# Attention with a feed-forward block in float32: values placed ahead of the scores from step 45 on, and the exponents of the weights formed in one ScalarE operation

## The chip, the cores and the metric

The kernel runs on one core of a Trainium2 chip. The time is device microseconds of one execution, from the first to the last instruction with what lies around them; lower is better. Three runs of the kernel before gave 1533.35, 1534.32 and 1534.38 us. One further execution was recorded by the profiler, and all durations below come from it.

## What is computed

Two blocks follow one another. The first is attention in which every query keeps the keys with its 32 largest scores; the second takes the rows of its result through a feed-forward pair of weights with `h - tanh(h)` between them.

```python
B, H, S, D = 8, 8, 576, 64
scores = scale * np.matmul(q, k.transpose(0, 1, 3, 2))
kth = np.partition(scores, -32, axis=-1)[..., -32:-31]
scores = np.where(scores >= kth, scores, -1e9)
attn = np.exp(scores - np.max(scores, axis=-1, keepdims=True))
attn = attn / (np.sum(attn, axis=-1, keepdims=True) + 1e-09)
x = np.matmul(attn, v)                       # -> (4608, 512)
h = x @ w_in                                 # w_in  (512, 2048)
g = h - np.tanh(h)
out = g @ w_out                              # w_out (2048, 512)
```

q, k and v are float32. The two weight matrices arrive as float64, as the inputs are set up, and are turned into float32 on the chip from their raw words.

## The kernel before

**Steps.** The attention is cut into 144 steps. A step takes 128 queries of two heads at once (a head pair; `t` in the code tells the two apart) against all 576 keys. Since 576 is four blocks of 128 and a rest of 64, every second head pair adds a step for the rests of two head pairs. There are 18 steps per batch. Steps of one unit (256 queries of a batch, or the rests of two batches) together give the rows that the feed-forward block needs.

**A step through the engines.** The work of step n is spread over several turns of the loop in `run`:

- `scores(n)` (L238): TensorE multiplies Q and K, eight passes of 288 columns, into the one score buffer `scps` in PSUM; ScalarE copies it to `sc` (L246). The next scores may be written only when L246 and the two VectorE reads L268 and L269 are done.
- `search(n)`: VectorE finds the 32nd largest score per row (L268 to L279, some 9 us per step). Between its rounds other VectorE work is slipped in: the turning of K and Q (L223), of the weights `z` (L388), and the conversion of the feed-forward matrices.
- `mask(n)` (L295 to L315) on ScalarE and GpSimd takes away what is below the threshold, `expo(n)` (L331) takes the exponential, `divide(n)` (L357) divides by the sum, `turn_z` and `spread_keys` (L388, L403, L405) bring the weights into key order by a VectorE transpose and a round trip through DRAM. In the first batch TensorE does this instead (`turn_pe`, L425, L428).
- `values(m)` (L453) multiplies the turned weights with V: 20 passes of 256 columns into `av`, which ScalarE copies into `xT` (L473). It runs for the last step of a group, five turns after that step (`LAG`). When this completes a unit, `work.extend(ffn(u))` puts the unit's feed-forward items into a list.

**Feed-forward items.** An item is a short run of matmuls, 1.7 us on TensorE: `ffn_h` (L504) for `w_in`, after every second item followed by tanh and a copy on ScalarE (L516, L517) and a difference on GpSimd (L518); and `ffn_o` (L525) for `w_out`, after every eighth item followed by a copy (L535) and the DMA out. In each turn of the loop `rate()` computes from the length of the list, and from when units fall due, how many items the turn should take, and `deal(part)` issues that share in parts: 0.4 ahead of the scores, then 0.2, 0.2 and 0.2 after them.

**Shapes on TensorE.** Feed-forward matmuls use the whole array (128*128 in the profile's notation). Scores use two tiles of 64 rows (64*128), values two tiles of 64 columns (128*64), each pair side by side.

**Order.** The order of the instructions on every engine is the order in which this loop issues them; nothing is rearranged later. Each engine then works through its own list and waits by semaphores where it needs something from another.

**The conversion.** `convert` takes one of 32 pieces (128 x 512 elements) from float64 to float32. Two DMAs bring the raw words and the same bytes shifted. VectorE cuts out the exponent field (L158) and the mantissa (L164), ScalarE turns both into numbers (L159 and L162 the exponent, L167 the mantissa), VectorE puts sign and exponent together (L170), GpSimd multiplies (L173). The pieces are spread over the searches of steps 0 to 10: two each in steps 0 and 1, three each in 2 to 9, four in step 10. A piece's exponent is clamped to the range 0 to 255 by two rectifiers in a row:

```python
nc.scalar.activation(f[:], fu, AF.Relu, bias=e1151[:], scale=-(2.0**23))
nc.scalar.activation(e.bitcast(I32), f[:], AF.Relu, bias=e255[:], scale=-1.0)
```

The kernel holds a second copy of the whole loop, with an exact search, which runs only if a count taken at the end of the first is above zero.

Of the kernel before, what the change touches and what calls it, by code (L numbers as in the profile page):

```python
# [8 lines left out]
AF = mybir.ActivationFunctionType  # L9
ALU = mybir.AluOpType  # L10
FP32 = mybir.dt.float32
I32 = mybir.dt.int32
# [6 lines left out]
EPS = 1.0e-9  # L19
J = 4  # L20
LAG = 5


class Step:
# [4 lines left out]
    def __init__(self, b, hp, qt, unit, col, i=0, nq=1, pe=False):  # L29
# [4 lines left out]

        self.lag = 2 if pe else LAG

# [13 lines left out]
def kernel(  # L50
# [9 lines left out]
    nc = tc.nc  # L60
    P = nc.NUM_PARTITIONS
# [15 lines left out]
    scale = 1.0 / float(D) ** 0.5  # L77
# [5 lines left out]
    def pool(name, bufs, **kw):  # L83
        return ctx.enter_context(tc.tile_pool(name=name, bufs=bufs, **kw))

    consts = pool("consts", 1)
# [28 lines left out]
    zx1 = consts.tile([P, 4 * S], FP32, name="zx")[:]  # L115
    et2 = [consts.tile([P, 4 * S], FP32, name="et")[:], later[:, 0 : 4 * S]]
    et_rem = later[:, 4 * S : 6 * S]
    e1151 = consts.tile([P, 1], FP32, name="e1151")
    nc.gpsimd.memset(e1151[:], 1151.0 * 2.0**23)
    e255 = consts.tile([P, 1], FP32, name="e255")  # L120
    nc.gpsimd.memset(e255[:], 255.0 * 2.0**23)

    def flat(x):
        return x.rearrange("p n w -> p (n w)")
# [13 lines left out]
    def convert(piece, slot):  # L138


        j, i = piece // CD, piece % CD
        if j < WJ:
            src, dst = moe_w_in[i * P : (i + 1) * P, j * NW : (j + 1) * NW], w_in[j][:, i, :]
        else:
            r0 = ((j - WJ) * FJ + i) * P
            src, dst = moe_w_out[r0 : r0 + P, :], w_out[j - WJ][:, i, :]
        raw, shifted, _ = slot
        nc.sync.dma_start(flat(raw), src.bitcast(U32))
        nc.sync.dma_start(
            flat(shifted).bitcast(U8)[:, 0 : 8 * NW - 4], src.bitcast(U8)[:, 3 : 8 * NW - 1]  # L150
        )
        yield
        hi = raw[:, :, 1]
        f = thpool.tile([P, NW], FP32, tag="th", name="f")
        fu = f[:].bitcast(U32)


        nc.vector.tensor_scalar(fu, hi, 20, 0x7FF, ALU.logical_shift_right, ALU.bitwise_and)  # L158
        nc.scalar.activation(f[:], fu, AF.Relu, bias=e1151[:], scale=-(2.0**23))  # L159

        e = h_ps.tile([P, NW], FP32, tag="h", name="e")[:] if j < WJ else f[:]
        nc.scalar.activation(e.bitcast(I32), f[:], AF.Relu, bias=e255[:], scale=-1.0)  # L162

        nc.vector.tensor_scalar(  # L164
            dst.bitcast(U32), shifted[:, :, 0], 0x0FFFFFFF, None, ALU.bitwise_and
        )
        nc.scalar.activation(dst, dst.bitcast(U32), AF.Copy, bias=1.0, scale=2.0**-28)  # L167
        yield

        nc.vector.scalar_tensor_tensor(  # L170
            out=fu, in0=hi, scalar=0x80000000, in1=e.bitcast(U32), op0=ALU.bitwise_and, op1=ALU.bitwise_or
        )
        nc.gpsimd.tensor_tensor(dst, dst, f[:], ALU.mult)  # L173
        yield
# [9 lines left out]
    def half(t):  # L184
        return slice(t * D, (t + 1) * D)
# [192 lines left out]
    def tiles(x, nq):  # L378

        x = x[:, 0 : nq * 2 * S]  # L380
        return x.rearrange("p (a k i j) -> p a k i j", a=NG, k=KC, j=G)
# [53 lines left out]
    def in_order(x, nq):  # L435

        return x.rearrange("p (a i j) -> p i a j", a=NG, i=nq)

    def values(n):


        g = steps[n]
        nq, u = g.nq, g.unit
        et = tiles(ets.pop(n), nq)
        w = nq * P
        av = zt_ps.tile([P, 2, N], FP32, tag="zt", name="av")
        for i in range(2 if g.rem else 1):
            cols = half(i) if g.rem else slice(0, w)
            es = et[:, 2 * i : 2 * i + 2] if g.rem else et
            hp = g.hp + i  # L450
            for c in range(J + 1):
                for t in range(2):
                    nc.tensor.matmul(  # L453
                        av[half(t), 0, cols],
                        vb[g.b, hp][:, t, c, :] if c < J else vr[g.b, hp][:, t, :],
                        es[:, :, (J + 1) * t + c if c < J else J].rearrange("p a i j -> p a (i j)"),
                        start=(c == 0),
                        stop=(c == J),
                    )
        if g.pe:  # L460
            rx = rxs.pop(n)
            for i in range(nq):
                nc.tensor.transpose(
                    in_order(av[:, 1, 0:w], nq)[:, i], rx[:, i].rearrange("p t d -> p (t d)"), ident[:]
                )
            xs = xrpool.tile([P, 2, N], FP32, tag="xs", name="xs")
            nc.scalar.copy(xs[:, :, 0:w], av[:, :, 0:w])

        def put(dst, order, cols):
            if g.pe:  # L470
                nc.gpsimd.tensor_tensor(dst, order(xs[:, 0, cols]), order(xs[:, 1, cols]), ALU.mult)
            else:
                nc.scalar.copy(dst, order(av[:, 0, cols]))  # L473

        if g.rem:
            for i in range(2):
                put(xt(u)[:, g.hp + i, g.col : g.col + R], lambda x: x, half(i))
        else:
            dst = xt(u)[:, g.hp, g.col : g.col + w].rearrange("p (i a j) -> p i a j", a=NG, i=nq)
            put(dst, lambda x: in_order(x, nq), slice(0, w))  # L480
        if n in done:
            work.extend(ffn(u))
# [3 lines left out]
    def xt(u):  # L486
        if u.xT is None:
            p = xpool if u.tag == "xT" else xrpool
            u.xT = p.tile([P, CD, N], FP32, tag=u.tag, name=u.tag)
        return u.xT  # L490
# [48 lines left out]
    def ffn(u):  # L539

        nh = CF * u.n // (2 * P)
        for item in range(nh):
            f = (item + 1) * CF // nh - 1
            yield CD * (f // FJ + 1), u, lambda item=item: ffn_h(u, item)
        for i in range(len(u.blocks)):
            for part in range(CF // 2):
                yield CD * (WJ + part // 2 + 1), None, lambda i=i, part=part: ffn_o(u, i, part)
# [3 lines left out]
    steps, done, work = [], {}, []  # L551
# [36 lines left out]
    def run(exact):  # L588
        plan()
        NS = len(steps)  # L590
# [7 lines left out]
        for i, (b, hp) in enumerate(pairs):  # L598
            n = next(n for n, g in enumerate(steps) if (g.b, g.hp) == (b, hp))
            for x, name in enumerate("kq"):  # L600
                m = max(n - 5 + x, turned.get(name, -4))
                if b == 0 and not exact:
                    m = -4
# [52 lines left out]
        def here(i):  # L656
            return 0 <= n + i < NS
# [26 lines left out]
        def rate():  # L684


            have, low, high = len(work), 0.0, None
            coming = sorted((t, u.n // 8) for u, t in ready.items() if t > n)
            for t, k in coming + [(NS + LAG, 0)]:
                r = have / max(t - n, 1)  # L690
                high = r if high is None else min(high, r)
                have += k
            for u, t in begun.items():
                if t > n and u in before:
                    need = [i + 1 for i, x in enumerate(work) if x[1] is before[u]]
                    if need:
                        low = max(low, need[-1] / (t - n))
            return max(low, high)
# [3 lines left out]
        def deal(part):  # L702
            nonlocal credit
            credit += part * share
            while work and credit > 0 and work[0][0] <= usable:
                work.pop(0)[2]()
                credit -= 1
            credit = min(credit, 1.0)

        for n in range(-4, NS + LAG):  # L710
            pe = here(-2) and steps[n - 2].pe
            for m in (n - LAG, n - LAG + 1, n - LAG + 2):
                if 0 <= m < NS and steps[m].last and steps[m].lag == n - m:
                    values(m)
            share, usable = rate(), converted[0]
            if pe:
                w = turn_pe(n - 2)
                next(w)
            if here(-1):
                mask(n - 1, exact)  # L720
            if here(0):
                search(n, exact, between)
            elif here(-2):
                between(0)
                between(LATE)
            if here(-2) and not pe and steps[n - 2].last:
                spread_keys(n - 2)
            if pe:
                spread(n - 2)
            deal(0.0 if pe else 0.4)  # L730
            if here(1):
                scores(n + 1)
            if pe:
                next(w)
            if here(-1):
                expo(n - 1)
            deal(0.8 if pe else 0.2)
            if pe and steps[n - 2].last:
                values(n - 2)
            deal(0.0 if pe else 0.2)  # L740
            for fn in todo.pop(n, []):
                fn()
            deal(0.2)
# [48 lines left out]
```

## Time and profile before

| | us |
|---|---|
| median of three runs | 1534.32 |
| the profiled execution | 1534.82 |
| its span (first to last instruction) | 1533.0 |
| TensorE (PE) busy | 1432.2 |
| VectorE (DVE) busy | 1349.9 |
| ScalarE (ACT) busy | 1021.6 |
| GpSimd (POOL) busy | 871.3 |
| last scores (step 143) begin on TensorE | 1408.59 |

How to read it: busy times overlap, so they don't add up to the span. A row of slices gives the busy share in 40 equal parts of the span, some 38 us each, in tenths. In the chain of waits each line is a piece of the work that ended last, with its start, its length and how many instructions it holds. PEld is the loading of weights into the array, which can lie beside matmuls. In a list of waits a line names the waiting instruction, what released it, the total, how often, and the longest.

### The profile page before, as it was taken

How to read it: one execution, taken by the hardware profiler on the slowest of the kernel's cores; microseconds unless marked ns; L12 is line 12 of the kernel's file. 1: busy time of each engine (PE TensorE's matmuls, PEld its weight loads, DVE VectorE, ACT ScalarE, POOL GpSimd, SP SyncE). 2: the span in 40 equal slices, each digit the busy share in tenths (PEclk: the TensorE clock that was granted, in tenths of full speed). 3: DMA queues.
4: the chain of work that ended last, by engine and by line, in shares of the span. 5: the costliest groups of instructions: out<-in, count | busy, mean ns of one | idle time of the engine just before them, and what ended most of it. 6: DMA issues, size and time to landing. Idle time of an engine off the chain costs nothing.

```text
span 1533.0 us, 24064 instructions
## 1 busy us (share of the span) xinstructions
PE 1432.2 (93%) x7302; PEld 901.9 (59%) x7302; DVE 1349.9 (88%) x3884; ACT 1021.6 (67%) x1833; POOL 871.3 (57%) x1371
## 2 busy tenths in 40 slices
PE   2567898999999999999999999999999999999997
PEld 1355566456465675656575665656565665656673
DVE  7998999999999999999999999999999999997100
ACT  4887777667676676767676676767676676767320
POOL 3777676656474564647474574647475574746210
PEclk9887999999999999999999999999999999999999
DMA  9944113556755666556655565556655666543400
GB/s 256 358 169 161 50 24 95 148 142 163 168 140 176 144 151 156 140 157 153 171 136 157 144 157 165 138 144 157 174 140 148 148 155 164 140 140 91 137 8 16
DMA packets 255467, 221.61 MB, mean 145 GB/s; under 512 B 197728, under 2 KB 204896, under 8 KB 248160
## 3 DMA queue, kind: packets, MB, share of 16 engines
q1 hardware_dynamic: 253552, 219.75, 53.4%
q8 instruction: 60, 0.98, 0.3%
q14 instruction: 79, 0.65, 0.2%
q10 hardware_dynamic: 1776, 0.22, 0.1%
HBM read 136.17 MB, written 83.76 MB: 143 GB/s over the span
## 4 chain that ended last, share of the span: by engine, by line
PE 75%; DVE 13%; ACT 5%; SPq 2%; DMA 2%; POOL 1%; issue 1%; DVEq 0%; ACTq 0%; POOLq 0%
PE ops L525 29%; PE hps L504 28%; PE av L453 9%; PE scps L238 8%; DVE m L276 3%; DVE ab L279 3%; DVE zx L388 2%; SPq L201 1%; DVE ab L269 1%; DVE ab L271 1%; DVE ab L268 1%; DMA zx<-in_moe_w_in_dram 1%; PE zt L425 1%; ACT z L308 1%; ACT sc L246 1%
## 5 line engine op out<-in xcount | busy, mean ns | idle before, releaser
L525 PE MATMUL ops<-w_out,g 128*128 128x512 f32 x1152 | 525.6, 603 | 0.0
L311 POOL TENSOR_TENSOR z<-sc,z 128x576 f32<-128x576 f32 x288 | 401.0, 1415 | 209.0 <-ACT z L308 209.0
L504 PE MATMUL hps<-xT,w_in 128*128 128x256 f32 (+1 forms) x2176 | 475.1, 374 | 0.5 <-ACT g L517 0.4
L276 DVE MAX8 m<-ab 128x8 f32<-128x288 f32 (+1 forms) x1152 | 468.4, 450 | 0.0
L504 PEld LDWEIGHTS hps<-xT,w_in 128*128 128x128 f32 x2176 | 391.6, 193 | 82.5 <-issue 32.3
L279 DVE MATCH_REPLACE8 ab<-m,ab 128x288 f32<-128x288 f32 x864 | 377.2, 446 | 0.0
L525 PEld LDWEIGHTS ops<-w_out,g 128*128 128x128 f32 x1152 | 211.3, 191 | 256.8 <-issue 240.6
L518 POOL TENSOR_TENSOR g<-g,th 128x512 f32<-128x512 f32 x144 | 182.8, 1274 | 159.3 <-ACT g L517 154.5
L308 ACT ACTIVATE z<-sc,tb 128x576 f32<-128x576 f32 x288 | 207.6, 769 | 89.7 <-POOL tb L295 78.2
L238 PE MATMUL scps<-kT,qT 64*128 64x288 f32 (+1 forms) x1280 | 188.2, 445 | 42.3 <-DVE qT L223 27.1
L331 ACT ACTIVATE z<-z,nb 128x576 f32<-128x576 f32 x288 | 221.2, 771 | 2.5 <-POOL z L311 2.4
L388 DVE STREAM_TRANSPOSE zx<-z 128x1152 f32<-128x1152 f32 x126 | 172.6, 1370 | 42.8 <-ACT z L357 42.5
L357 ACT ACTIVATE z<-z,rd 128x576 f32<-128x576 f32 x252 | 180.3, 763 | 44.3 <-DVE rd L350 44.3
L238 PEld LDWEIGHTS scps<-kT,qT 64*128 64x128 f32 (+1 forms) x1280 | 102.3, 184 | 130.4 <-issue 42.4
L246 ACT COPY sc<-scps 128x1152 f32<-128x1152 f32 x144 | 159.2, 1105 | 11.3 <-PE scps L238 10.2
L341 POOL TENSOR_SCALAR rd<-den 128x2 f32<-128x2 f32 x144 | 33.5, 233 | 198.6 <-ACT z L331 197.6
L516 ACT ACTIVATE th<-hps 128x512 f32<-128x512 f32 x144 | 84.8, 589 | 89.9 <-PE hps L504 87.5
L268 DVE TENSOR_TENSOR ab<-scps,sc 128x576 f32<-128x576 f32 x144 | 105.7, 734 | 13.9 <-ACT sc L246 6.5
L271 DVE MAX8 ab<-ab 128x8 f32<-128x288 f32 x288 | 116.2, 445 | 0.0
L269 DVE TENSOR_TENSOR ab<-scps,sc 128x576 f32<-128x576 f32 x144 | 107.4, 746 | 0.0
L453 PE MATMUL av<-et,vb 128*64 128x256 f32 (+1 forms) x640 | 77.2, 373 | 30.4 <-ACT et L428 30.4
L535 ACT COPY ot<-ops 128x512 f32<-128x512 f32 x36 | 21.0, 584 | 114.3 <-PE ops L525 114.3
(70 smaller groups left out, 1157.5 us busy)
## 6 DMA issues: line engine op xcount, KB each, us to landing
there<-zx SPq DMA_DIRECT2D x56, 1152.0 KB, 4.2
spare<-there SPq DMA_DIRECT2D x112, 288.0 KB, 5.3
et<-there SPq DMA_DIRECT2D x112, 288.0 KB, 5.1
kin<-in_k_dram SPq DMA_DIRECT2D x116, 72.0 KB, 2.4
vb<-in_v_dram SPq DMA_DIRECT2D x64, 128.0 KB, 5.7
out_dram<-ot SPq DMA_DIRECT2D x32, 256.0 KB, 2.3
qin<-in_q_dram SPq DMA_DIRECT2D x113, 72.0 KB, 3.1
there<-zx SPq DMA_DIRECT2D x14, 576.0 KB, 4.8
```

The lines of the kernel that those rows point to most:

```text
L238: nc.tensor.matmul(ps[rows, t, s, 0:S2], qT[g.b, g.hp + i][half(t), qs], kT[g.b, g.hp + i][half(t), ks], start=True, stop=True,)
L276: nc.vector.max(m[:, t, m8], last[t] if i == rounds - 1 else cur[t])
L279: nc.vector.match_replace(nxt[t], m[:, t, m8], cur[t], NEG)
L308: nc.scalar.activation(zv[:, t, :], scf[:, t, :], AF.Relu, bias=tb[:, t : t + 1], scale=-BIG)
L311: nc.gpsimd.tensor_tensor(zv[:, t, :], scf[:, t, :], zv[:, t, :], ALU.subtract)
L331: nc.scalar.activation(x["zv"][:, t, :], x["zv"][:, t, :], AF.Exp, bias=x["nb"][:, t : t + 1], scale=scale, accum_out=den[:, t : t + 1],)
L357: nc.scalar.activation(x, x, AF.Copy, scale=rds[n][:, g.i, t : t + 1])
L388: nc.vector.transpose(tiles(zx, g.nq)[:, :, :, g.i, :].rearrange("p c k j -> p k c j"), z[:].rearrange("p (k c j) -> p k c j", c=NG, j=G),)
L453: nc.tensor.matmul(av[half(t), 0, cols], vb[g.b, hp][:, t, c, :] if c < J else vr[g.b, hp][:, t, :], es[:, :, (J + 1) * t + c if c < J els ...
L504: nc.tensor.matmul(cur[u][:, s : s + w], w_in[j][:, c, fo : fo + P], u.xT[:, c, 0:w], start=(c == 0), stop=(c == CD - 1),)
L518: nc.gpsimd.tensor_tensor(g, g, th[:], ALU.subtract)
L525: nc.tensor.matmul(cur[u][:], u.g[o // 1024][:, o % 1024 // 512, o % 512 : o % 512 + P], w_out[f // FJ][:, f % FJ, :], start=(f == 0), sto ...
```

## The change

There are two parts.

First, `values` of a step is issued at another place. Up to step 44 it stays at the start of the loop's turn. From turn 45 (`NEAR`) on it is issued after the first `deal`, directly ahead of `scores(n + 1)`. The call also stands after `rate()` then.

Second, the exponent of a converted piece is formed by one rectifier from the integer field, where there were two. The lower clamp at 0 stays; the upper clamp at 255 is gone.

```diff
+NEAR = 45
...
-    e1151 = consts.tile([P, 1], FP32, name="e1151")
-    nc.gpsimd.memset(e1151[:], 1151.0 * 2.0**23)
-    e255 = consts.tile([P, 1], FP32, name="e255")
-    nc.gpsimd.memset(e255[:], 255.0 * 2.0**23)
+    e896 = consts.tile([P, 1], FP32, name="e896")
+    nc.gpsimd.memset(e896[:], -896.0 * 2.0**23)
...
         nc.vector.tensor_scalar(fu, hi, 20, 0x7FF, ALU.logical_shift_right, ALU.bitwise_and)
-        nc.scalar.activation(f[:], fu, AF.Relu, bias=e1151[:], scale=-(2.0**23))

         e = h_ps.tile([P, NW], FP32, tag="h", name="e")[:] if j < WJ else f[:]
-        nc.scalar.activation(e.bitcast(I32), f[:], AF.Relu, bias=e255[:], scale=-1.0)
+        nc.scalar.activation(e.bitcast(I32), fu, AF.Relu, bias=e896[:], scale=2.0**23)
...
             pe = here(-2) and steps[n - 2].pe
-            for m in (n - LAG, n - LAG + 1, n - LAG + 2):
-                if 0 <= m < NS and steps[m].last and steps[m].lag == n - m:
-                    values(m)
+            def due():
+                for m in (n - LAG, n - LAG + 1, n - LAG + 2):
+                    if 0 <= m < NS and steps[m].last and steps[m].lag == n - m:
+                        values(m)
+
+            if n < NEAR:
+                due()
             share, usable = rate(), converted[0]
...
             deal(0.0 if pe else 0.4)
+            if n >= NEAR:
+                due()
             if here(1):
                 scores(n + 1)
```

## The prediction

> **What bounds the kernel now.** I read the page first (busy shares and the 40 slices), then busy time by stretch, then the chain of waits in order of time, since matmul busy time alone proves little for pipelined work.
>
> ```profile
> PE 1432.2 (93%) x7302; PEld 901.9 (59%) x7302; DVE 1349.9 (88%) x3884; ACT 1021.6 (67%) x1833; POOL 871.3 (57%) x1371
> PE   2567898999999999999999999999999999999997
> DVE  7998999999999999999999999999999999997100
> ```
>
> ```profile
> 400.00:500.00 100.00, 97.50 (x501) 60.57 (x501) 100.00 (x292) 69.13 (x125) 55.78 (x91) 1.00 0.61 162
> 600.00:800.00 200.00, 200.00 (x976) 126.78 (x974) 193.43 (x557) 140.86 (x254) 120.21 (x192) 1.00 0.58 150
> ```
>
> The columns are the stretch, its length, busy PE, PEld, DVE, ACT, POOL. From 200 to about 434 us VectorE has no gap and sets the pace. After that TensorE has none, and VectorE keeps 3 to 4% spare: two engines nearly tied, so a gain on one soon meets the other. The chain shows what TensorE does there (start, length, what):
>
> ```profile
> 464.17 1.17 PE scps L238 x8
> 465.34 7.06 PE ops L525 x16
> 472.40 1.17 PE scps L238 x8
> 473.58 5.35 PE ops L525 x12
> 478.92 2.31 PE av L453 x20
> 481.23 1.91 PE ops L525 x4
> 483.15 1.17 PE scps L238 x8
> 484.32 5.35 PE ops L525 x12
> ```
>
> No piece waits for another engine. The price to read off is that of changing the kind of matmul. Four `ops` matmuls cost 1.72 us in a pure run (509.15 to 510.87 in the same chain); twelve after scores cost 5.35, not 5.16; sixteen cost 7.06, not 6.88; four after values cost 1.91. So the first feed-forward (FF) piece after another kind pays 0.19 us. Scores and values pay on entry too. In a pure run a column costs 1.72 us / (4 x 512) = 0.84 ns; scores and values run as pairs of tiles side by side, so half of that. Scores: 8 x 288 x 0.42 ns = 0.97 us, against 1.17, which leaves 0.20. Values: 20 x 256 x 0.42 ns = 2.15, against 2.31, which leaves 0.16.
>
> How far TensorE is from waiting on VectorE:
>
> ```profile
> 477.63 0.76 DVE L269 TENSOR_TENSOR ab<-scps,sc 128x576 f32<-128x576 f32 x1
> 483.08 1.24 PE L238 MATMUL scps<-kT,qT 64*128 64x288 f32 x8
> ```
>
> L269 is the last reader of the one score buffer; the next scores may start when it ends (478.39) and start 4.7 us later. Read in the same way up to step 139, this lead lies between 2.2 and 6.3 us. It is what TensorE may gain locally before it has to wait.
>
> The conversion of the weights runs in steps 0 to 10 (a step begins with L268 on VectorE):
>
> ```profile
> L159 ACT ACTIVATE f<-f,e 128x512 f32<-128x512 uint32 x32 | 22.7, 711 | 11.1 <-DVE f L158 11.1
> L162 ACT ACTIVATE e<-f,e 128x512 int32<-128x512 f32 x16 | 11.1, 692 | 0.6
> ```
>
> ```profile
> 49.07:99.16 50.09, 30.47 (x190) 22.50 (x186) 47.90 (x138) 44.94 (x83) 38.08 (x53) 0.80 0.72 262
> 99.16:163.18 64.02, 43.77 (x248) 32.34 (x248) 52.56 (x139) 49.97 (x91) 46.41 (x57) 0.81 0.45 162
> ```
>
> ```profile
> DVE f L170 <- ACT f L162: 10.9, 4, 4.6
> ```
>
> Here VectorE idles 2.2 us in the first stretch (steps 3 to 6) and 11.5 in the second (7 to 10); 10.9 of the latter are four waits for an exponent. ScalarE is 90% busy in the first stretch, VectorE 96%.
>
> **What the Trainium skill says.** "TensorEngine Tiling (Array Packing)", Key Properties: changing the tiling mode, not just the tile, drains TensorE. The trace agrees: L504 and L525 run 128*128, L453 128*64, L238 64*128, and each change costs 0.16 to 0.20 us. "ScalarE: Activation LUTs", What ACT_TABLE_LOAD costs: an ACTIVATE with a pointer bias takes 280 ns + 0.833 per element, an estimate of 706 for 512; the trace has 711 and 692 to 722. "PSUM — Partial Sum Buffer", Engine vs sequencer instructions: ScalarE's queue is strictly first in, first out; so a copy waiting for values holds up what is queued behind it, and L473 after L453 idles 71.8 us between 500 and 1400 us.
>
> **Part 1: one ScalarE operation per piece.** Removed: 32 instructions of 711 ns, 0.74 us from start to start. The remaining one keeps its price (integer input as L159, integer output as L162). Of the 23 us most lie beside VectorE work. Steps 3 to 6 turn in 12.2 to 12.7 us, with only some 0.5 us of VectorE idle each: with ScalarE 2.2 us faster per step VectorE takes over, so I count the idle, 2.0 us. In steps 7 to 10 the loop is L170 (third piece), GpSimd L173 and rx, TensorE, ScalarE et and mask, first exponent, L170 (first piece); only the first piece's L159 lies on it: 4 x 0.74 = 3.0. In step 10 a late second exponent, after a VectorE wait for its load, may add 0.6; I leave that for the range. Sum -5.0 us. Bounds: 0 if VectorE or the loads fill every gap; -9 if all L159 time on the chain counts (8.6% of 84 to 165 us is 7.0, plus the 2.0). Afterwards VectorE, then TensorE run gapless to the end, so an earlier start carries through. One constant less on GpSimd (0.1 us at the start) is nothing: ScalarE and VectorE wait for loads there.
>
> **Part 2: values right ahead of scores.** Before, a step with values runs FF, values, FF, scores. After it runs FF, values, scores. Counting both orders, 55 steps lose one run of FF as a separate piece, so 313 kind changes become 258. Gone per step: values to FF (0.19) and FF to scores (0.20). New: values to scores, which no row of this trace shows. Below: 0, if one drain serves. Above: 0.39, if leaving the one tiling and entering the other each cost one. I take 0.20, the price of entering scores from FF: 55 x 0.19 = -10.5 us. No matmul is added or removed.
>
> What moves with it. `work.extend` now comes after `rate()`, so in the step that completes a unit the share is computed without that unit's FF items: two or three items (1.72 each) are missing there and come later, five (8.7 us) only after the last scores. TensorE pays for them either way, unless it runs into the score buffer in the thin steps. I ran two sums forward: scores start at the later of TensorE's own work and the end of L269; VectorE's next step starts at the later of 2.85 us after the scores began (1.24 matmuls, 1.10 copy, hand-over) and 8.82 us after its previous start, 9.48 where it also turns K or Q (375.95 to 385.44 in its timeline). The old order gives no wait, as in the trace. The new one gives 3.1 us, mainly where two thin steps meet (before the scores of steps 59 and 60). With 4.0 instead of 2.85 it is 5.5 us, with 5.0 it is 11. Taken +3; range +1 to +6.
>
> ScalarE: L473 now queues just before the score copy, and mask (L308) and divide (L357) no longer stand behind it. The second tanh and copy of a run (0.58 + 0.57 us) now follow divide, ahead of the score copy, and run beside values or scores. The later FF needs xT only after the scores, 1.2 us: hidden. GpSimd's mask product starts earlier, its tanh difference later; it is 60% busy. VectorE's order and SP's DMA order stay; DMAs into V remainders and et wait for values that are one FF piece (1.7 us) later, with steps of 9.6 us in hand. Uncovered, one such wait costs what it exceeds the step by; taken at 0.
>
> **Sum.** Span 1533.0 - 5.0 - 10.5 + 3.0 = 1520.5. The profiled execution took 1534.82, 1.8 above its span, and 0.5 above the median of 1534.32: 1520.5 + 1.8 - 0.5 = 1521.8 us.
>
> **Rivals.**
> - A, the change costs only once (values to scores near 0): 55 x 0.39 = -21.5 us, but TensorE then leans on VectorE and the two sums give 6 us of waits: 1533.0 - 5 - 21.5 + 6 + 1.3 = 1513.8. For: both kinds are two-tile modes. Against: every change here costs about the same.
> - B, early gain covered: VectorE fills the conversion stage, part 1 gives 0 to -1, and thin steps cost 5: 1533.0 - 0.5 - 10.5 + 5 + 1.3 = 1528.3. For: only 2 us of VectorE idle in steps 3 to 6. Against: the four waits of 10.9 us end exactly on L162.
> - C, values to scores costs 0.39, both drains: switching gains nothing, early gain stays, waits of 1: 1533.0 - 5 + 1 + 1.3 = 1530.3. For: neither of the two tilings contains the other. Against: 0.19 into and out of the full array look like one exposed weight load.
> - D, slower: the direct change between a column-split and a row-split array costs 0.65 us. Then 55 x (0.65 - 0.39) = +14.3, minus 5.0: 1533.0 + 9.3 + 1.3 = 1543.6. It ends slower by 0.2% from 0.54 us on (55 x 0.15 = 8.1 = 5.0 + 3.1). Against it: nothing here pays half of that.
> - E, order not as described: excluded for the order itself, which I counted; that step 45 falls before TensorE is the bound is excluded by the chain, gapless from 434 us, step 45 being near 468.
>
> **Numbers.** Chances: forecast 0.54, A 0.14, B 0.15, C 0.11, D 0.06. Range 1511 to 1530: from A's full early gain to C. The 0.2% that can be told is 3.1 us: faster below 1531.2. C, with some 2 us to either side, splits about evenly over that line, and D is slower: faster 0.54 + 0.14 + 0.15 + 0.05 = 0.88, within 0.06, slower 0.06.
>
> **What would show it.** Chain after 470 us: values followed at once by scores, the scores still about 1.17 us (A: below 1.0; C: 1.4; D: 1.6). L268 of step 12, now at 170.8 us, near 166. The last scores, now at 1408.6, near 1387 (-5 - 10.5 + 3 - 8.7), the tail 8.7 us longer. TensorE gaps before the scores of steps 59 and 60 with VectorE's L269 as releaser. I am wrong if the values-to-scores price differs, if gaps add up to over 6 us, or if step 12 starts where it did.

## The result, and the profile after

The changed kernel took 1527.24 us (median of six runs, 1525.71 to 1528.04) against 1533.62 for the kernel before (six runs, 1532.89 to 1534.38): a ratio of 0.9956 with a 95% interval of 0.9944 to 0.9969. It is faster by 6.4 us where 12.5 were forecast.

Line numbers from L157 on are smaller by one or two after the change: L268 is now L266, L238 is L236, L504 and L525 are L502 and L523, L170 is L168. The head of the page after, with its slices:

```profile
PE 1420.7 (93%) x7302; PEld 904.1 (59%) x7302; DVE 1350.9 (89%) x3884; ACT 1002.3 (66%) x1801; POOL 875.1 (57%) x1370
PE   2577898999999999999999999999999999999998
DVE  7998999999999999999999999999999999887000
```

PE is busy for 11.5 us less with the same number of matmuls; 10.5 of that is the forecast's sum for fewer changes of kind. ScalarE lost its 32 instructions. The chain of waits of the kernel after, around steps 45 to 47 (start, length, what):

```profile
468.77 1.17 PE scps L236 x8
469.94 7.06 PE ops L523 x16
477.01 2.31 PE av L451 x20
479.32 1.17 PE scps L236 x8
480.49 5.35 PE ops L523 x12
```

Values (`av`) are followed at once by scores, and these take 1.17 us, as they did after feed-forward work. So the new change of kind, values to scores, costs what the forecast took for it, 0.20 us. Over all steps from 45 on that issue values, the time that TensorE's own work doesn't explain has a median of 0.02 us when each change is priced at 0.19. Rivals A, C and D each needed another price and fall here.

Busy time by stretch (stretch, length, busy PE, PEld, DVE, ACT, POOL):

```profile
600.00:800.00 200.00, 197.89 (x990) 127.64 (x989) 198.95 (x577) 144.40 (x261) 120.50 (x192) 1.00 0.64 158
```

In the same stretch before, PE was busy for all of the 200 us and DVE for 193.43. TensorE now stands still for 2.1 us, and VectorE has 1 us to spare in 200. The list of TensorE's waits from 430 to 1500 us, empty in the kernel before between 500 and 1400 (waiting instruction, what released it, total, times, longest):

```profile
PE scps L236 <- DVE ab L267: 2.3, 2, 1.2
PE ops L523 <- POOL bad L313: 1.2, 1, 1.2
PE hps L502 <- ACT ot L533: 1.1, 1, 1.1
PE ops L523 <- POOL rd L339: 0.9, 1, 0.9
PE hps L502 <- ACT g L515: 0.9, 1, 0.9
```

The first line is the forecast wait at the scores of steps 59 and 60. The other four, 4.1 us, were not in the forecast: it is a feed-forward matmul that waits, before a tile of the PSUM pool `h_ps`, which serves `hps` and `ops` alike (called `h` tiles below). The engine named as releaser is not always the one that matters, as the timeline of the second of these shows (start, length, engine, line, what, idle time before):

```profile
502.28 1.06 PE L502 MATMUL hps<-xTr,w_in 128*128 128x128 f32 x8
...
503.27 1.24 PE L236 MATMUL scps<-kT,qT 64*128 64x288 f32 x8
...
503.41 1.44 ACT L306 ACTIVATE z<-sc,tb 128x576 f32<-128x576 f32 x2 [0.75 <-POOL tb L293]
...
504.44 2.05 PE L502 MATMUL hps<-xTr,w_in 128*128 128x128 f32 x16
...
505.21 1.44 ACT L355 ACTIVATE z<-z,rd 128x576 f32<-128x576 f32 x2 [0.36 <-DVE rd L348]
...
506.55 0.57 ACT L514 ACTIVATE th<-hps 128x512 f32<-128x512 f32 x1
...
507.03 0.57 ACT L515 COPY g<-hps 128x512 f32<-128x512 f32 x1
...
507.70 1.53 PE L523 MATMUL ops<-w_out,g 128*128 128x512 f32 x3 [1.21 <-POOL bad L313]
```

`h_ps` has two tiles. Both are full when TensorE comes to L523 at 506.5. The tile that it needs is freed by L515, which ends at 507.60, 0.1 us before L523 starts; GpSimd's L313 happens to end at that time too. L514 and L515 are late because they stand behind mask (L306) and divide (L355) in ScalarE's queue. Before the change values, 2.3 us of TensorE work that needs no `h` tile, stood by the order of issue between the feed-forward items of such a run and left ScalarE that much more time.

The waits of steps 45 to 143 together, as what TensorE's own work leaves unexplained, were 1.87 us before and are 9.44 after: 7.6 more, 2.5 of it at the score buffer (steps 59, 60), 5.2 at `h` tiles (ahead of the scores of steps 51, 79, 81 and 94; the list above counts the idle time alone). The last scores begin at 1393.3 us, 15.3 earlier; five feed-forward items, 8.6 us, moved behind them.

For the conversion, VectorE's waits for the exponent in steps 7 to 10 fell from the 10.9 us shown before to:

```profile
DVE f L168 <- ACT f L160: 6.7, 4, 3.0
```

Yet L266 of step 12 starts at 168.1 us, only 2.6 earlier, and step 45 is 3.6 earlier.

### The profile page after: what moved, and what is told of

Read it like the earlier page. It is cut to its first block, busy times and chain, and to the rows that moved or that the text cites. A ratio compares the mean times of both kernels' runs of the same rounds, so it can differ in the third digit from the quotient of the medians.

```text
span 1525.7 us, 24089 instructions
## 1 busy us (share of the span) xinstructions
PE 1420.7 (93%) x7302; PEld 904.1 (59%) x7302; DVE 1350.9 (89%) x3884; ACT 1002.3 (66%) x1801; POOL 875.1 (57%) x1370
## 4 chain that ended last, share of the span: by engine, by line
PE 62%; DVE 26%; ACT 4%; POOL 3%; issue 2%; SPq 1%; DMA 1%; DVEq 0%; ACTq 0%; POOLq 0%
PE hps L502 24%; PE ops L523 24%; PE av L451 7%; DVE m L274 7%; DVE ab L277 7%; PE scps L236 7%; DVE zx L386 3%; DVE ab L267 2%; DVE ab L269 2%; DVE ab L266 2%; SPq L199 1%; DVE f L157 1%; POOL z L309 1%; ACT z L306 1%; DVE f L168 1%
## 5 line engine op out<-in xcount | busy, mean ns | idle before, releaser
L523 PE MATMUL ops<-w_out,g 128*128 128x512 f32 x1152 | 517.7, 600 | 2.1 <-POOL bad L313 1.2
L502 PE MATMUL hps<-xT,w_in 128*128 128x256 f32 (+1 forms) x2176 | 467.2, 372 | 2.5 <-ACT g L515 1.2
L502 PEld LDWEIGHTS hps<-xT,w_in 128*128 128x128 f32 x2176 | 392.4, 192 | 78.0 <-issue 21.9
L523 PEld LDWEIGHTS ops<-w_out,g 128*128 128x128 f32 x1152 | 213.3, 191 | 262.5 <-issue 248.6
L306 ACT ACTIVATE z<-sc,tb 128x576 f32<-128x576 f32 x288 | 207.7, 769 | 146.4 <-POOL tb L293 131.6
L355 ACT ACTIVATE z<-z,rd 128x576 f32<-128x576 f32 x252 | 180.8, 764 | 101.6 <-DVE rd L348 101.5
L236 PE MATMUL scps<-kT,qT 64*128 64x288 f32 (+1 forms) x1280 | 190.6, 449 | 44.8 <-DVE qT L221 27.2
L386 DVE STREAM_TRANSPOSE zx<-z 128x1152 f32<-128x1152 f32 x126 | 171.9, 1364 | 16.2 <-ACT z L355 16.1
L236 PEld LDWEIGHTS scps<-kT,qT 64*128 64x128 f32 (+1 forms) x1280 | 103.6, 185 | 122.5 <-issue 49.9
L266 DVE TENSOR_TENSOR ab<-scps,sc 128x576 f32<-128x576 f32 x144 | 105.3, 731 | 28.9 <-ACT sc L244 24.0
L514 ACT ACTIVATE th<-hps 128x512 f32<-128x512 f32 x144 | 84.3, 585 | 64.4 <-PE hps L502 62.0
L267 DVE TENSOR_TENSOR ab<-scps,sc 128x576 f32<-128x576 f32 x144 | 107.1, 744 | 0.0
L293 POOL TENSOR_SCALAR tb<-m 128x1 f32<-128x1 f32 x288 | 88.4, 316 | 6.9
```

The lines of the kernel that those rows point to most:

```text
L236: nc.tensor.matmul(ps[rows, t, s, 0:S2], qT[g.b, g.hp + i][half(t), qs], kT[g.b, g.hp + i][half(t), ks], start=True, stop=True,)
L306: nc.scalar.activation(zv[:, t, :], scf[:, t, :], AF.Relu, bias=tb[:, t : t + 1], scale=-BIG)
L355: nc.scalar.activation(x, x, AF.Copy, scale=rds[n][:, g.i, t : t + 1])
L386: nc.vector.transpose(tiles(zx, g.nq)[:, :, :, g.i, :].rearrange("p c k j -> p k c j"), z[:].rearrange("p (k c j) -> p k c j", c=NG, j=G),)
L502: nc.tensor.matmul(cur[u][:, s : s + w], w_in[j][:, c, fo : fo + P], u.xT[:, c, 0:w], start=(c == 0), stop=(c == CD - 1),)
L523: nc.tensor.matmul(cur[u][:], u.g[o // 1024][:, o % 1024 // 512, o % 512 : o % 512 + P], w_out[f // FJ][:, f % FJ, :], start=(f == 0), sto ...
```

## The experiments

Every run is given with its median, and with its ratio to the kernel before as measured beside it on the same chip.

**The two parts alone.** First the exponent with `NEAR` out of reach, so that values stay at the old place; then the kernel before with nothing but the new place of values.

```diff
-NEAR = 45
+NEAR = 999
```

> The exponent edit alone; values stay at the start of the turn in all steps. Theory: the start of step 12 comes 3.6 us earlier, as in the changed kernel, and everything behind it shifts by that: 1530.0 us against 1533.6, the four VectorE waits for an exponent near 6.7 us. Rival 1 (the two parts depend on each other): below 1528 or above 1532. Rival 2, as forecast: 5.0 us less, 1528.6.

> The placing of values alone; both rectifiers stay. Theory: 55 changes of kind less give -10.5 us, and six waits of TensorE of 0.9 to 1.5 us, with some smaller ones, give back about 7.5: -3, near 1530.5. Rival, as forecast: waits of 3, so -7.5, 1526.1. If the price of values to scores were the cause, the scores pieces after values would last longer than 1.17 us.

Exponent alone: 1532.15 us, ratio 0.9991 (0.9983 to 1.0000), a gain of 1.4 us, with no TensorE wait listed after 430 us. Values alone: 1530.47 us, 0.9980 (0.9973 to 0.9987), 3.1 us, with all the waits above. That is what the terms give: 10.5 us saved at the changes of kind less 7.6 of waits is 2.9. Both parts were worth less than the forecast's 5.0 and 7.5.

The traces show the second part more sharply than the medians. From the scores of step 45 to its last matmul, TensorE takes 1060.6 us in all four profiles with values at the old place (the kernel before, exponent alone, and two runs below) and 1057.6 us in all four with values at the new place and nothing else altered behind step 45 (the change twice, values alone, and one run below). So the new place is worth 3.0 us there, with the exponent edit or without it, and some 0.8 us more behind the last matmul (8.4 us to the end before, 7.6 after). What differs between profiles of one kernel lies ahead of step 45. What follows looks at each of the two shortfalls.

**Are thin steps the cause of the waits?** `rate()` counts the items of a unit that completes in the same turn, as it did when values came first. Values stay ahead of the scores.

```diff
+        def falling(n):
+            ms = (n - LAG, n - LAG + 1, n - LAG + 2)
+            return [m for m in ms if 0 <= m < NS and steps[m].last and steps[m].lag == n - m]
...
             have, low, high = len(work), 0.0, None
+            if n >= NEAR:
+                have += sum(done[m].n // 8 for m in falling(n) if m in done)
```

> The changed kernel, with the share of a turn computed as if the unit completed in that turn were already in the list; no matmul added or left out. No thin steps at units' ends any more, and the five items are back ahead of the last scores. Theory (thin steps cause all the waits, those on the score buffer and those on the feed-forward buffer): -3.6 - 10.5 and no waits above 0.5 us after 430 us: 1519.5 to 1521. Rival (ScalarE's new order makes the waits, thin steps only the two on the score buffer): 2.4 us better than the changed kernel, 1524.8, the other four waits still there in other places.

1532.85 us, 0.9997 (0.9989 to 1.0005): no gain left at all. The list of TensorE's waits:

```profile
PE hps L502 <- ACT g L515: 6.1, 7, 0.9
PE ops L523 <- POOL rd L339: 2.6, 3, 0.9
```

The score-buffer waits are gone, as the theory said, and in their place stand waits at `h` tiles, 13.6 us of unexplained time in all. So thin steps make only the waits at the score buffer. Those at `h` tiles come more often without thin steps; the reading, which the waits alone don't prove, is that an even share leaves more turns with a long unbroken run of items. The timeline of ScalarE and TensorE at one of these waits:

```profile
622.96 1.44 ACT L306 ACTIVATE z<-sc,tb 128x576 f32<-128x576 f32 x2 [1.67 <-POOL tb L293]
624.30 1.43 ACT L355 ACTIVATE z<-z,rd 128x576 f32<-128x576 f32 x2
625.63 1.10 ACT L244 COPY sc<-scps 128x1152 f32<-128x1152 f32 x1
...
628.16 0.58 ACT L514 ACTIVATE th<-hps 128x512 f32<-128x512 f32 x1
628.64 0.57 ACT L515 COPY g<-hps 128x512 f32<-128x512 f32 x1
```

```profile
622.94 5.45 PE L502 MATMUL hps<-xT,w_in 128*128 128x256 f32 x24
629.27 1.99 PE L502 MATMUL hps<-xT,w_in 128*128 128x256 f32 x8 [0.88 <-ACT g L515]
```

Mask, divide, score copy and exponential hold ScalarE from 622.96 to 628.16 without a gap; in that time TensorE fills what tiles there are and waits for the end of L515 at 629.21.

**Feed-forward ahead of the mask.** If the tanh and copy come too late behind mask and divide, the first `deal` may be issued ahead of them.

```diff
+            if n >= NEAR and not pe:
+                deal(0.4)
             if here(-1):
                 mask(n - 1, exact)
...
-            deal(0.0 if pe else 0.4)
+            deal(0.0 if pe or n >= NEAR else 0.4)
```

> The changed kernel, with the first share of a turn issued ahead of mask, so that on ScalarE tanh and copy of feed-forward stand ahead of mask and divide again; TensorE's list is that of the changed kernel, thin steps too. Theory (evacuation behind mask and divide makes the four waits on the feed-forward buffer): these four go, 4.1 us, the two on the score buffer stay: about 1523. Rival (thin steps alone make them): no change within 1 us of 1527.2. Against the theory's gain: mask then waits for tanh, so VectorE may wait more for divided weights.

A miss, and the wrong way: 1542.36 us, 1.0056 (1.0042 to 1.0070). TensorE's two largest waits, and VectorE's largest:

```profile
PE scps L236 <- DVE ab L267: 7.9, 7, 2.0
PE hps L502 <- ACT g L515: 7.4, 9, 0.9
DVE zx L386 <- ACT z L355: 55.2, 28, 11.7
```

Now mask and divide stand behind a tanh that waits for TensorE, and VectorE's turning of the weights (L386) waits for divide (L355): 55.2 us, where it was 16.1 in the changed kernel. VectorE falls behind, and the scores wait for its L267. At `h` tiles nothing is gained. So this run doesn't separate the new order on ScalarE from the missing values as the reason why the tiles are emptied too late.

**The changed kernel once more**, on the chip of the next three edits:

> The changed kernel once more, beside the others on one chip. The two parts alone gave 1.5 and 3.2 us; added they give 4.7, against the 6.4 of the first measurement. If the parts just add up, 1529; if they help each other, 1527.

1527.72 us, 0.9955 (0.9942 to 0.9969), 6.9 us faster. In this profile step 45 starts only 0.2 us earlier than in that of before, where the first profile of the same kernel showed 3.6. One profile can't place the start of step 45 to better than some 3 us; the medians must do that.

**A third buffer.** From turn 45 on, every third `h` tile is taken from the PSUM pool that values use: once with the even share, once in the changed kernel as it is.

```diff
+    def h_tile():
+        taken[0] += 1
+        if at_turn[0] >= NEAR and taken[0] % 3 == 0:
+            return zt_ps.tile([P, 512], FP32, tag="zt", name="hps")
+        return h_ps.tile([P, 512], FP32, tag="h", name="hps")
...
-                cur[u] = h_ps.tile([P, 512], FP32, tag="h", name="hps")
+                cur[u] = h_tile()
```

> The even share of e3 (share counts the unit that completes), and from turn 45 on every third tile of h in PSUM taken from the two buffers of the values, so three feed-forward tiles can be open at a time. TensorE's order is that of e3. Theory (a run of four items fills both buffers of h while ScalarE is at mask, divide, score copy and exponential, so the third tile waits): the eleven waits of some 1.1 us in e3 go, -11.7, so 1521. Rival (the waits come from somewhere else, as the score copy or V): stays at 1532.9. Against it: values may now wait for a tile of h, up to 1 us each.

> The changed kernel with the third buffer of e6 and nothing else; thin steps as in the changed kernel. Theory: the four waits on a buffer of h (1.49, 1.43, 1.15, 1.16 at the scores of steps 51, 79, 81, 94) go, -4 to -5; the two at 59 and 60 on the score buffer stay: 1522.5. Rival (thin steps make them): no change.

With the even share: 1526.94 us, 0.9948 (0.9935 to 0.9962). Against the even share with two buffers the ratio falls by 0.0049, or 7.5 us, and the unexplained time of TensorE falls by the same 7.5, from 13.6 to 6.0. That shows that the `h` buffers were what TensorE waited for. The expected 1521 was missed all the same: it counted on 11.7 us of waits, and 7.5 went. Of the longer waits these stay (L529 is L523 here), before tiles for `ops`, which keep the two buffers:

```profile
PE ops L529 <- POOL rd L339: 2.8, 3, 0.9
```

In the changed kernel the third buffer gives nothing that the times show: 1527.98 us, 0.9955 (0.9941 to 0.9968). Two of the four `h` waits are gone (steps 51 and 81), but TensorE then comes to the scores of step 59 earlier, and there VectorE isn't ready:

```profile
PE scps L236 <- DVE ab L267: 3.8, 2, 2.6
```

It was 2.3, with 1.2 the longest. Over half of the time gained at one buffer is waited out at the other. Thin steps and full `h` tiles are two limits in a row. From the scores of step 45 to the last matmul the traces have 1061.8 us with the even share, 1056.4 with the third buffer and 1054.3 with both, against 1057.6 in the changed kernel. So the third buffer alone gains 1.2 us there, and more with the even share than without it. The median with both, 1526.94 against 1527.72, is within the scatter of the runs, which lies ahead of step 45.

**The conversion.** Why is part 1 worth 1.4 us where VectorE's exponent waits fell by more? The timelines of before and after, in the same step (GpSimd's mask product, then VectorE's second half of one piece and first half of the next):

```profile
54.42 2.78 POOL L311 TENSOR_TENSOR z<-sc,z 128x576 f32<-128x576 f32 x2 [0.94 <-ACT z L308]
56.37 0.69 DVE L170 SCALAR_TENSOR_TENSOR f<-w_out,e 128x512 uint32<-128x512 uint32 x1 [0.61 <-ACT e L162]
56.97 0.52 DVE L158 TENSOR_SCALAR f<-w_out 128x512 uint32<-128x512 uint32 x1
57.41 0.41 DVE L164 TENSOR_SCALAR w_in<-w_out 128x512 uint32<-128x512 uint32 x1
```

```profile
54.01 2.78 POOL L309 TENSOR_TENSOR z<-sc,z 128x576 f32<-128x576 f32 x2 [0.98 <-ACT z L306]
55.22 0.67 DVE L168 SCALAR_TENSOR_TENSOR f<-w_out,e 128x512 uint32<-128x512 uint32 x1
55.81 1.25 DVE L157 TENSOR_SCALAR f<-w_out 128x512 uint32<-128x512 uint32 x1
56.99 0.41 DVE L162 TENSOR_SCALAR w_in<-w_out 128x512 uint32<-128x512 uint32 x1
```

Counted from the start of GpSimd's product, the second half starts at 1.95 us before and at 1.21 after: the 0.74 of the removed operation. But the next first half now starts while GpSimd is at work and lasts until the product is done, 1.25 us in place of 0.52. The operation after it starts at 2.99 us before and at 2.98 after: the gain is given back to within 0.01 us. The second half just ahead of it, whose exponent lies in PSUM, is not held up: 0.67 us within the same product. Over the kernel this first operation (L158, then L157) grew from 15.0 to 22.8 us in 32 pieces; by shapes, in steps 3 to 6 of before and of after (instructions, busy us, mean ns):

```profile
L158 DVE TENSOR_SCALAR f<-w_out 128x512 uint32<-128x512 uint32 x8 | 3.5, 441 | 0.0
L158 DVE TENSOR_SCALAR f<-spare 128x512 uint32<-128x512 uint32 x3 | 1.4, 483 | 0.0
```

```profile
L157 DVE TENSOR_SCALAR f<-w_out 128x512 uint32<-128x512 uint32 x8 | 5.0, 619 | 0.0
L157 DVE TENSOR_SCALAR f<-spare 128x512 uint32<-128x512 uint32 x3 | 3.3, 1101 | 0.0
```

Steps 3 to 6 and 7 to 10 after the change, in the columns used above for busy time by stretch:

```profile
48.62:99.27 50.65, 30.28 (x184) 22.40 (x184) 50.03 (x138) 37.05 (x72) 41.83 (x53) 0.76 0.76 263
99.27:160.54 61.27, 42.22 (x248) 30.73 (x248) 54.53 (x140) 39.92 (x75) 48.47 (x57) 0.83 0.49 170
```

Against the two stretches before, VectorE's idle time fell by 6.3 us, more than the forecast's 5.0. Its busy time grew by 4.1: 7.8 more in the first operation, less 3.2 that the second halves lost. That leaves 2.2 us in this profile, and steps 3 to 6 even became 0.6 us longer.

The Trainium skill has a reason for the longer operation, "SBUF — State Buffer", Who interferes with whom: VectorE's `tensor_scalar` in a two-port mode shares a pair of ports with GpSimd, and whichever issues first holds it while the other blocks fully. The trace agrees with the blocking: VectorE's instruction ends only after GpSimd's. That ports are the cause is the skill's word; the traces show the overlap.

To take this overlap away, the first halves of all three pieces of steps 2 to 9 are put into the first round of the search, ahead of the first second half.

```diff
-            for k in mine[1:]:
-                seq += [(1, k), (2, k - 1)]
-            seq += [(2, k) for k in mine[-1:]]
+            if len(mine) == 3:
+                seq += [(1, k) for k in mine[1:]] + [(2, k) for k in mine]
+            else:
+                for k in mine[1:]:
+                    seq += [(1, k), (2, k - 1)]
+                seq += [(2, k) for k in mine[-1:]]
...
-                at_round.setdefault((m, 3 * i // max(len(seq) - 1, 1)), []).append(
+                r = max(0, i - 2) if len(mine) == 3 else 3 * i // max(len(seq) - 1, 1)
+                at_round.setdefault((m, r), []).append(
```

> The changed kernel with the conversion's VectorE order altered in steps 2 to 9: the exponent and mantissa fields of all three pieces are cut out in the first round, ahead of the first L168, where the third piece's stood behind it. Theory (VectorE's third L157, 1.25 us in place of 0.41, waits for GpSimd's mask product L309 to end): the third one takes 0.41 again, some 0.7 us in each of steps 3 to 6 and perhaps in 7 to 9: -2 to -4 us at the start of step 12. Rival (VectorE is the bound by its own instructions): unchanged, or slower because ScalarE's third exponent waits for a free buffer.

1522.20 us, 0.9920 (0.9906 to 0.9933), 5.5 us less than the changed kernel on the same chip. L157 takes its short time again in steps 3 to 6:

```profile
L157 DVE TENSOR_SCALAR f<-w_out 128x512 uint32<-128x512 uint32 x8 | 3.3, 415 | 0.0
L157 DVE TENSOR_SCALAR f<-spare 128x512 uint32<-128x512 uint32 x3 | 1.2, 416 | 0.0
```

Over the kernel it takes 17.1 us, 5.7 less, about the gain of 5.5. Steps 3 to 6 show it best: VectorE is idle for 0.6 us there in either kernel, the operation takes 3.7 us less, and the stretch is 3.8 us shorter. The new order might be worth this by itself, so it was also put into the kernel before, and into the one with the exponent alone:

> The kernel before, with its two exponent operations and its values at the old place, and only the order of the conversion halves changed in steps 2 to 9 as in the run of first halves together. Theory: with two ScalarE operations a piece ScalarE is what the conversion stage waits for, the third bit operation meets GpSimd's product only at its end (0.41 to 0.5 us instead of 1.25), so there is little for this edit to save: within 1.5 us of before, 1532 to 1535 us. Rival: the order of the halves is worth its 5.5 us by itself, with the exponent edit or without: 1528 us.

> The exponent by one ScalarE operation and the first halves of all three pieces together, values at the old place. Theory: the exponent edit's forecast 5 us were withheld by VectorE's bit operation standing behind GpSimd's product; with that out of the way the exponent edit is worth 5 us or more over the kernel that has the halves alone, so 1526 to 1528 us here against 1532 to 1535 there. Rival: the exponent edit is worth the 1.5 us that it brought alone, whatever the order: 1.5 us under the kernel with the halves alone.

| | exponent as before | one operation |
|---|---|---|
| halves as before | 1 | 0.9991 (0.9983 to 1.0000) |
| first halves together | 0.9993 (0.9984 to 1.0001) | 0.9946 (0.9932 to 0.9959) |

In medians 1533.35 and 1526.82 us for the lower row, which was measured on another chip than the upper. By the ratios the exponent alone is worth 1.4 us, the order alone 1.1, both together 8.3; by the medians 1.5, 0.8 and 7.4. So with the first halves together the exponent edit is worth 0.0047 x 1534 = 7.2 us, or 6.5 by the medians. The rival, in which the order brings its 5.5 us anyway, falls.

The kernel before with the first halves together isn't free of overlap, though; there it falls on GpSimd:

```profile
67.59 3.64 POOL L311 TENSOR_TENSOR z<-sc,z 128x576 f32<-128x576 f32 x2 [1.38 <-ACT z L308]
```

VectorE's bit operations were under way when this product began and kept their 0.43 us each; the product took 3.64 us in place of 2.78. That happens in three of steps 3 to 6. What it costs there wasn't measured, so some of the 7.2 us may be owed to it.

**All together**: even share, third buffer and first halves.

> The changed kernel with three edits tried singly so far: a feed-forward share that counts the unit completing in the same turn, a third of the h tiles in the zt buffer from turn 45 on, and in steps 2 to 9 the first halves of all three conversion pieces ahead of the second halves. If the two gains are separate, one in steps 2 to 10 and one from step 45 on, they add: 1526.9 (share and third buffer) less 5.5 (first halves together) gives 1521.4 us. Rival: an earlier start makes VectorE the bound again between steps 12 and 60, or the score buffer takes back what the h buffers give; then it is no better than the first halves alone, 1522.2 us or above.

1522.86 us, 0.9920 (0.9907 to 0.9934): as fast as the first halves alone, and the rival was nearer. Its trace has 6.1 us of unexplained TensorE time against 9.4, and from the scores of step 45 to the end of the span it takes 1063.0 us against 1065.1 with the first halves alone. Profiles with the same order behind step 45 agree in this time to 0.1 us, so the 2.1 us are there; the median doesn't show them, as the runs scatter over 4 us. The first halves in the changed kernel beat both kernels, and by the least edit.

## Why the prediction was right in sign and half in size

- **The price of a change of kind.** Confirmed: values to scores costs 0.20 us, and 55 changes less are worth the 10.5 us of the forecast.
- **Waits of +3 us (range to 6).** This term failed: 7.6. The two sums run forward knew only the score buffer, and there they were good: steps 59 and 60 as named, 2.5 us where 3.1 had been worked out. (VectorE's spare time, read as 3 to 4%, was 7% from 1200 to 1400 us; nothing hangs on that.) The rest is the step of the forecast that the second tanh and copy "now follow divide, ahead of the score copy, and run beside values or scores", taken at no cost. It asked who needs `xT`, and not when the two `h` tiles become free. TensorE fills two tiles and reaches a third in less time than ScalarE takes from mask to copy: 5.2 us in four places. The runs with a third buffer show that the tiles were what was waited for.
- **The conversion, -5.0 us.** This term failed too: -1.4 alone. The idle time that it counted does go. "With ScalarE 2.2 us faster per step VectorE takes over, so I count the idle" took VectorE's own work as given, and that grew by 4.1 us in steps 3 to 10, since the first operation slid under GpSimd's product (+7.8). The forecast had a lower bound of 0 for loads or VectorE filling the gaps, not for VectorE itself becoming slower. With the first halves together the edit is worth 7.2 us, within the forecast's bound of 9.
- **The sum.** -1.4 - 10.5 + 7.6 = -4.3, against 6.4 measured. The parts alone, 1.4 and 3.1, add to 4.5; the intervals of the three ratios, about 1 us to either side for each part and 2 for the whole, cover the difference of 1.9. The traces show no help of one part to the other from step 45 on; whether there is any ahead of it stays open. That 1527.24 lies within the stated 1511 to 1530 owes something to luck: the upper end was set by rival C, whose price for values to scores was wrong.
- **Of the rivals** B had the mechanism (early gain covered, waits of 5) and gave 1528.3, nearer than the forecast's 1521.8; but what covers the early gain is a slower VectorE, and most of the waits are at `h` tiles, not in thin steps.

## What to carry to other kernels

Work that stands between two runs of another kind also gives the buffers of those runs time to be emptied; before closing such a gap to save switches, count the tiles of the longest run and the queue of the engine that empties them. When an operation is taken out ahead of an instruction, look at what that instruction will now overlap: an engine's own durations aren't constants. An edit that brings next to nothing alone isn't yet refuted: by the ratios the exponent edit and the order of the halves brought 1.4 and 1.1 us alone, and 8.3 together.

## What the runs showed of the hardware

A VectorE `tensor_scalar` on 128 x 512 uint32 of 0.41 us takes 1.25 us when it starts within GpSimd's product of two SBUF operands: it ends 0.27 us after the product, whose own 2.78 us don't change. Where such VectorE operations were already under way, it was the product that grew, to 3.64 us. VectorE's second half with its exponent in PSUM took 0.67 us within the same product. On TensorE, going straight from a column-split to a row-split array costs the same 0.20 us as going there from the full array.
